# Second chunk's rows loaded uncast between the weight quarters, rows re-ordered at their cast, weight halves crossed over in bf16, work of the first step re-ordered

## The chip, the cores and the metric

The kernel runs on one core of a Trainium2 chip. The metric is the device time of one execution in microseconds (us). Every run quoted is of state fast unless it says otherwise, and its mean granted TensorE clock is given where it matters. PE is the matmul engine, DVE the vector engine, ACT the scalar engine, POOL is GpSimd, SP issues DMAs. A DMA lands when its data have arrived. An eviction is the copy that takes a result of PE to where the next operation reads it.

## The reference

```python
# x: (8, 4096, 192) fp32; weight: (8 heads, 7 taps); w_in: (192, 2048); w_out: (2048, 192); beta: (2048,)
w = exp(weight - max); w = w / (sum(w) + 1e-9)            # softmax over the 7 taps of a head
conv = causal 7-tap convolution of x along the sequence, one set of taps per head of 24 columns
h = conv @ w_in
out = (h * sigmoid(beta * h)) @ w_out                     # 32768 x 192, fp32
```

## The kernel before

The batch is worked in two halves side by side, in steps. Steps 0 and 1 are the two half-chunks (256 tokens) of chunk 0; step 2 is chunk 1 (512 tokens), and so on to step 32. A step has 16 units; a unit multiplies one block of 128 hidden columns (`hidden`), lets ACT apply the activation, and does a quota of output matmul pairs. From chunk 2 on, x comes transposed through DRAM. For the first two chunks that would be too late, so they are transposed on PE:

```python
    x0 = setup.tile([128, NB, 2, D], FP32)      # chunk 0, loaded fp32 by SP
    x0b = setup.tile([128, NB, 2, D], BF16)
    x1b = setup.tile([128, NB, 2, D], BF16)     # chunk 1, cast to bf16 by its DMA
    ...
    def load_x1(h):                             # issued from POOL after the first weight cast
        nc.gpsimd.dma_start(out=x1b[:, :, h, :], in_=x_v[0, TOK : 2 * TOK, h, :].rearrange(...))
    ...
    def cast_w_in(i):                           # POOL: half of weight quarter i
        nc.gpsimd.tensor_copy(w_in_s[:, :, i*FW : i*FW + FH], w_in_raw[:, :, i, :])
    def cross_w_in(i):                          # DVE: the other half, moved across partitions
        for r in range(2):
            nc.vector.tensor_copy(
                w_in_s[(1 - r)*DG : (2 - r)*DG, :, i*FW + FH : (i+1)*FW],
                w_in_raw[r*DG : (r+1)*DG, :, i, :])
    def scale_w_out(i):                         # POOL, right behind cast_w_in(i): 128 x 768 multiply
        ...
    # one transpose for each 64-column group AND each half: 6 for a block of 128 tokens
```

Chunk 0 is convolved on PE with diagonal matrices (7 matmuls a column group). Chunk 1 and all later ones are convolved on DVE: 21 taps a step (7 taps for each of three groups of 64 columns; a tap is one DVE instruction), popped from a queue between the units. What is slipped into the units of step 0 is given by a table:

```python
    first_work = {
        0: lambda: (first_xt(), cross_w_in(1)),
        2: more(xt1_work),              # chunk 1: transposes of its first two blocks
        3: lambda: cross_w_in(2),
        4: more(xt1_work),              # chunk 1: the other two, and the copy to xt
        6: more(conv1_work),            # chunk 0, second half: convolution on PE, group by group
        7: lambda: cross_w_in(3),
        8: more(conv1_work),
        11: more(conv1_work),
    }
    quota = {0: 2, 1: 4, 2: 6, 3: 6, 4: 7}   # output pairs per unit, 8 from step 5 on
    pops = {0: 8, 1: 14, 2: 26}              # DVE taps popped in a step
```

Of the kernel before, what the change touches and what calls it, by code (L numbers as in the profile page):

```python
# [9 lines left out]
FP32 = mybir.dt.float32  # L10
FP32R = mybir.dt.float32r
BF16 = mybir.dt.bfloat16
AF = mybir.ActivationFunctionType
ALU = mybir.AluOpType
# [3 lines left out]
def kernel(  # L18
# [17 lines left out]
    nc = tc.nc  # L36

    B, S, D = x.shape
    H, K = weight.shape
    F = moe_w_in.shape[1]  # L40
    group = D // H
    DG = 64
    NG = D // DG
    TOK = 512
    NF = F // 128
    PAD = K - 1
    HALO = 16
    BLK = 128
# [8 lines left out]
    x_v = x.rearrange("(h p) s d -> p s h d", h=2)  # L57
    out_v = out.rearrange("(h p s) d -> h p s d", h=2, p=B // 2)

    consts = ctx.enter_context(tc.tile_pool(name="consts", bufs=1))  # L60
    setup = ctx.enter_context(tc.tile_pool(name="setup", bufs=1))
# [13 lines left out]
    psum_b = ctx.enter_context(  # L75
        tc.tile_pool(name="psum_b", bufs=1, space=bass.MemoryType.PSUM)
    )
# [3 lines left out]
    def in_a():  # L81
        return psum_a.tile([128, 2, TOK], FP32, name="pa")

    def in_b():
        return psum_b.tile([128, 2, TOK], FP32, name="pb")
# [3 lines left out]
    def new_xt(ch):  # L89
        xt = xt_pool.tile([128, NG, HALO + TOK], BF16, name="xt")  # L90
        if ch % CHUNKS == 0:
            nc.vector.memset(xt[:, :, 0:HALO], 0.0)
        xts[ch] = xt
        return xt
# [22 lines left out]
    NB = TOK // BLK  # L117
    HB = NB // 2
    x0 = setup.tile([128, NB, 2, D], FP32)
    x0b = setup.tile([128, NB, 2, D], BF16)  # L120
    x1b = setup.tile([128, NB, 2, D], BF16)



    NW = 4
    FW = F // NW
    FH = FW // 2
    NQ = NF // NW
    w_in_s = consts.tile([128, NG, F], BF16)
    w_in_raw = setup.tile([128, NG, NW, FH], FP32)  # L130
# [2 lines left out]
    w_in_v = moe_w_in.rearrange("(c d) (i r f) -> i r d c f", c=NG, r=2, f=FH)  # L133
    w_out_v = moe_w_out.rearrange("(c p) d -> p c d", p=128)

    def load_x0(b):
        nc.sync.dma_start(out=x0[:, b, :, :], in_=x_v[0, b * BLK : (b + 1) * BLK, :, :])  # L137

    def load_w_in(i):
        for r in range(2):  # L140
            nc.sync.dma_start(  # L141
                out=w_in_raw[r * DG : (r + 1) * DG, :, i, :], in_=w_in_v[i, r]
            )
# [2 lines left out]
        fcs = slice(i * NQ, (i + 1) * NQ)  # L146
        nc.sync.dma_start(out=w_out_raw[:, fcs, :], in_=w_out_v[:, fcs, :])

    def load_x1(h):
        nc.gpsimd.dma_start(  # L150
            out=x1b[:, :, h, :],
            in_=x_v[0, TOK : 2 * TOK, h, :].rearrange("(b q) d -> q b d", q=BLK),
        )

    e8 = setup.tile([H, K + 1], FP32)
    cw8 = setup.tile([H, K], FP32)
    beta_q = setup.tile([NF, 128], FP32)
    nc.scalar.dma_start(out=cw8, in_=weight)
    nc.scalar.dma_start(out=beta_q, in_=moe_beta.rearrange("(c p) -> c p", p=128))
    for b in range(HB):  # L160
        load_x0(b)
    load_w_in(0)
    load_w_out(0)
    for b in range(HB, NB):
        load_x0(b)
    for i in range(1, NW):
        load_w_in(i)
        load_w_out(i)

# [6 lines left out]
    sel = setup.tile([H, NG, 2, DG], FP32)  # L176
# [3 lines left out]
        out=sel,  # L180
        in_=sel,
        compare_op=ALU.is_ge,
        fill=0.0,
# [5 lines left out]
        out=sel,  # L189
        in_=sel,  # L190
        compare_op=ALU.is_ge,
        fill=0.0,
# [4 lines left out]
    ident = setup.tile([128, 128], FP32)  # L197
# [3 lines left out]
    def cast_w_in(i):  # L201
        nc.gpsimd.tensor_copy(  # L202
            w_in_s[:, :, i * FW : i * FW + FH], w_in_raw[:, :, i, :]
        )

    def cross_w_in(i):
        for r in range(2):
            nc.vector.tensor_copy(  # L208
                w_in_s[(1 - r) * DG : (2 - r) * DG, :, i * FW + FH : (i + 1) * FW],
                w_in_raw[r * DG : (r + 1) * DG, :, i, :],  # L210
            )

    def w_in_of(h, j, fc):
# [7 lines left out]
    def scale_w_out(i):  # L221
        fcs = slice(i * NQ, (i + 1) * NQ)
        nc.gpsimd.tensor_tensor(  # L223
            w_out_s[:, fcs, :],
            w_out_raw[:, fcs, :],
            beta_r[:, fcs].unsqueeze(2).to_broadcast((128, NQ, D)),
            ALU.mult,
        )
# [6 lines left out]
    nc.scalar.activation(warm, warm, AF.Silu)  # L235
    ident_b = setup.tile([128, 128], BF16)
    nc.vector.tensor_copy(ident_b, ident)
    pf = psum_h.tile([128, 2, TOK], FP32, name="ph")

    def fill(n):  # L240
        for _ in range(n):
            nc.tensor.matmul(pf[:, 0, :], zeros[:, 0:128], zeros, start=True, stop=True)  # L242

    fill(5)
    pq = in_a()[:, 0, 0 : NG * (K + 1)]
    for c in range(NG):
        nc.tensor.matmul(
            pq[:, c * (K + 1) : (c + 1) * (K + 1)],
            sel[:, c, :, :].rearrange("i h d -> i (h d)"),
            e8,  # L250
            start=True,
            stop=True,
        )
    pq = pq.rearrange("p (c k) -> p c k", c=NG)
    fill(1)
    nc.vector.tensor_copy(x0b[:, 0], x0[:, 0])
    rq = setup.tile([128, NG], FP32)
    nc.vector.reciprocal(rq, pq[:, :, K])
    cw = consts.tile([128, NG, K], FP32)
    nc.vector.tensor_tensor(  # L260
        cw, pq[:, :, 0:K], rq.unsqueeze(2).to_broadcast((128, NG, K)), ALU.mult
    )
    nc.vector.tensor_copy(x0b[:, 1], x0[:, 1])

    diag = setup.tile([128, NG, K, 128], FP32R)

    def diag_v(c):
        nc.vector.tensor_tensor(
            diag[:, c, :, :],
            ident.unsqueeze(1).to_broadcast((128, K, 128)),  # L270
            cw[:, c, :].unsqueeze(2).to_broadcast((128, K, 128)),
            ALU.mult,
        )

    def transposes(pt, xb, b0, at, nb):
        for b in range(nb):
            for c in range(NG):
                for h in range(2):
                    nc.tensor.transpose(  # L279
                        pt[h * DG : (h + 1) * DG, c, (at + b) * BLK : (at + b + 1) * BLK],  # L280
                        xb[:, b0 + b, h, c * DG : (c + 1) * DG],
                        ident_b,
                    )

    xt0 = setup.tile([128, NG, HALO + TOK], FP32R)
    nc.vector.memset(xt0[:, :, 0:HALO].bitcast(FP32), 0.0)
    cts = {}
# [12 lines left out]
    n0 = HB * BLK  # L300
    for b in range(HB):
        pool, name = (psum_b, "pb") if b == 0 else (psum_a, "pa")
        pt = pool.tile([128, NG, BLK], BF16, name=name)
        transposes(pt, x0b, b, 0, 1)
        nc.scalar.copy(xt0[:, :, HALO + b * BLK : HALO + (b + 1) * BLK], pt)
    pb = in_b()[:, 0, 0:NF]
    nc.tensor.transpose(pb, beta_q, ident[0:NF, 0:NF])
    fill(1)
    diag_v(0)
    diag_v(1)  # L310
    beta = consts.tile([128, NF], FP32)
    nc.vector.tensor_copy(beta, pb)
    nc.vector.reciprocal(beta_r, beta)
    for k in range(K):
        nc.scalar.mul(diag[:, 2, k, :], ident, cw[:, 2, k : k + 1])
    cross_w_in(0)
    cast_w_in(0)
    for h in range(2):
        load_x1(h)
    scale_w_out(0)  # L320
    for i in range(1, NW):
        cast_w_in(i)
        scale_w_out(i)
    ct = ct_pool.tile([128, NG, TOK], BF16, name="ct")
    cts[0] = ct
    for c in range(NG):
        pv = psum_h.tile([128, 2, TOK], FP32, name="ph") if c < 2 else in_a()
        pv = pv[:, 0, 0:n0]
        for k in range(K):
            diag_tap(0, c, k, pv)  # L330
        if c < 2:
            nc.vector.tensor_copy(ct[:, c, 0:n0], pv)
        else:
            nc.scalar.copy(ct[:, c, 0:n0], pv)
    nc.vector.tensor_copy(x0b[:, HB:NB], x0[:, HB:NB])

    def first_xt():
        pt = psum_b.tile([128, NG, n0], BF16, name="pb")
        transposes(pt, x0b, HB, 0, HB)
        nc.vector.tensor_copy(xt0[:, :, HALO + n0 :], pt)  # L340

    def first_conv():
        cts[1] = ct_pool.tile([128, NG, TOK], BF16, name="ct")
        pv = psum_b.tile([128, 4, n0], FP32, name="pb")
        for c in range(NG):
            for k in range(K):
                diag_tap(1, c, k, pv[:, c, :])
            if c == NG - 1:
                nc.vector.tensor_copy(cts[1][:, :, 0:n0], pv[:, 0:NG, :])  # L349
            yield  # L350

    def second_xt():
        xt = new_xt(1)
        pt = psum_b.tile([128, NG, TOK], BF16, name="pb")
        for b in range(NB):
            transposes(pt, x1b, b, b, 1)
            if b % 2 == 0:
                continue
            if b == NB - 1:
                nc.vector.tensor_copy(  # L360
                    xt[:, :, HALO - PAD : HALO], xt0[:, :, HALO + TOK - PAD :]
                )
                nc.vector.tensor_copy(xt[:, :, HALO:], pt)  # L363
            yield

    cast(2)
    cast(3)
# [124 lines left out]
    def more(work):  # L492
        return lambda: next(work, None)

    first_work = {
        0: lambda: (first_xt(), cross_w_in(1)),
        2: more(xt1_work),
        3: lambda: cross_w_in(2),
        4: more(xt1_work),
        6: more(conv1_work),  # L500
        7: lambda: cross_w_in(3),
        8: more(conv1_work),
        11: more(conv1_work),
    }



    quota = {0: 2, 1: 4, 2: 6, 3: 6, 4: 7}
    pops = {0: 8, 1: 14, 2: 26}
    queue = deque()  # L510
    for s in range(N_ST):
        if s + 2 < N_ST:
# [48 lines left out]
```

## Time and profile before

| | before |
|---|---|
| time, median (4 runs) | 704.49 us (704.37 to 705.06) |
| the traced run | 701.91 us, mean granted clock 0.998 |
| PE / DVE / ACT busy, share of the span | 98% / 79% / 83% |
| first unit of step 2 reaches ACT (timeline) | 44.87 us |

From 45 us on PE is busy almost all the time (45 to 100 us: 54.71 of 55); what can still be won is the start. These are lines of the chain of waits of the kernel before (start, duration, what), followed back from the matmul that opens step 2:

```profile
8.39 10.32 DMA x1b<-in_x_dram
...
18.75 0.85 PE pb L279 x11
...
28.27 1.04 PE pb L292 x7
...
29.34 0.96 DVE ct L349
30.30 3.31 DVE ct L382 x5
...
34.67 4.63 DVE ct L382 x7
...
40.36 2.05 DVE ct L382 x4
...
42.93 1.42 DVE ct L382 x2
44.34 0.04 issue
44.38 0.39 PE ph L398 x2
```

Read upwards: step 2's first hidden group is completed at 44.38 by the last DVE taps (L382); they stand in line behind the eviction of chunk 0's convolution (L349), that behind PE's last convolution group (L292), and that behind the transposes of chunk 1 (L279), which waited for the cast-DMA of x1b until 18.7 us.

The windows view of the same kernel shows what the wait did to PE (columns: window, busy time and count of PE, PE's weight loads, DVE, ACT, POOL, then granted clock, DMA share, GB/s):

```profile
core 0: us, PE busy (x) PEld busy (x) DVE busy (x) ACT busy (x) POOL busy (x), PEclk, DMA share, GB/s
14.30:18.75 4.45, 0.24 (x1) 0.11 (x2) 4.18 (x5) 0.55 (x1) 2.35 (x3) 0.95 1.23 249
18.75:22.06 3.31, 3.31 (x43) 2.33 (x45) 0.00 (x0) 1.38 (x2) 2.59 (x3) 0.56 0.24 64
```

PE worked 0.24 of 4.45 us, and then ran at a clock of 0.56. Three lines of the timeline of before (start, duration, engine, what, and in brackets the idle time before it):

```profile
17.11 1.47 POOL L223 TENSOR_TENSOR w_out_s<-w_out_raw,beta_r 128x768 bf16<-128x768 f32 x1 [1.83 <-DMA w_out_raw<-in_moe_w_out_dram]
17.29 1.31 DVE L360 CAST xt<-xt 128x18 bf16<-128x18 f32 x1
18.75 0.85 PE L279 MATMUL pb<-ident_b,x1b 128*64 128x128 bf16 x11 [2.92 <-DMA x1b<-in_x_dram]
```

The middle line is a copy of 18 elements that took 1.31 us: it ended when POOL's multiply ended. And the group of the crossing on the page of before, eight instructions of 0.9 us in the mean (the copy, its shapes, count, then busy us and mean ns):

```profile
L208 DVE CAST w_in_s<-w_in_raw 64x768 bf16<-64x768 f32 x8 | 7.2, 905 | 0.2
```

### The profile page before, as it was taken

The numbers are of one execution on the slowest core, as the hardware profiler recorded it, in microseconds if no ns is written. First come the engines' busy times: TensorE is split into PE (matmuls) and PEld (weight loads), VectorE is DVE, ScalarE is ACT, GpSimd is POOL, SyncE is SP. The second block draws the span as 40 slices with busy tenths as digits, with TensorE's granted clock in tenths as the row PEclk, the third lists the DMA queues.
The fourth block names the chain that finished last, engine by engine and source line by source line (L and its number), as shares of the span: only waits on it lengthen the run. The fifth ranks groups of instructions, "written<-read, shape, count | busy, mean of one in ns | idle before, by whom it ended". The sixth has DMA issues, their size and how long they took to land.

```text
span 700.2 us, 25076 instructions
## 1 busy us (share of the span) xinstructions
PE 688.7 (98%) x11464; PEld 504.6 (72%) x11464; DVE 554.1 (79%) x938; ACT 580.5 (83%) x546; POOL 67.5 (10%) x79
## 2 busy tenths in 40 slices
PE   7999999999999999999999999999999999999997
PEld 5776677777777777777777777777777777777777
DVE  7699999989779877779877778877778977777222
ACT  4689998888888888888888888888888888888882
POOL 5835454000000000000000000000000000000000
PEclk9999999999999999999999999999999999999999
DMA  9999999922231222321223221232221322211111
GB/s 220 124 165 167 166 174 174 143 59 65 65 59 45 62 59 70 58 60 47 58 61 70 59 60 49 57 58 70 60 59 56 50 63 66 60 44 39 37 47 59
DMA packets 184955, 55.38 MB, mean 79 GB/s; under 512 B 147456, under 2 KB 184848, under 8 KB 184848
## 3 DMA queue, kind: packets, MB, share of 16 engines
q0 software_dynamic: 96768, 12.53, 27.8%
q1 hardware_dynamic: 88032, 41.24, 25.4%
q8 instruction: 89, 1.46, 0.9%
q14 instruction: 18, 0.15, 0.1%
q10 hardware_dynamic: 48, 0.01, 0.0%
HBM read 28.98 MB, written 37.29 MB: 95 GB/s over the span
## 4 chain that ended last, share of the span: by engine, by line
PE 94%; DVE 2%; DMA 2%; issue 0%; SPq 0%; ACT 0%; POOL 0%; POOLq 0%
PE ph L398 46%; PE pa L426 24%; PE pb L426 24%; DVE ct L382 2%; DMA x1b<-in_x_dram 1%; DMA w_in_raw<-in_moe_w_in_dram 1%; PE pb L292 0%; DVE osb L445 0%; DVE osb L444 0%; PE pb L279 0%; DVE ct L349 0%; SPq L137 0%; POOL w_in_s L202 0%; SPq L141 0%; ACT g L405 0%
## 5 line engine op out<-in xcount | busy, mean ns | idle before, releaser
L405 ACT ACTIVATE g<-ph,beta 128x1024 bf16<-128x1024 f32 (+1 forms) x528 | 573.3, 1088 | 101.4 <-PE ph L398 95.2
L426 PEld LDWEIGHTS <-g 64*128 64x128 bf16 x8192 | 354.2, 94 | 119.6 <-issue 0.8
L398 PE MATMUL ph<-ct,w_in_s 64*128 64x512 bf16 (+1 forms) x3168 | 419.5, 370 | 0.7 <-DVE ct L382 0.3
L382 DVE SCALAR_TENSOR_TENSOR ct<-xt,cw,ct 128x512 bf16<-128x512 bf16 x558 | 377.2, 744 | 0.0
L426 PE MATMUL pa<-w_out_s,g 64*128 64x192 bf16 x4128 | 217.2, 243 | 0.9 <-issue 0.6
L426 PE MATMUL pb<-w_out_s,g 64*128 64x192 bf16 x4064 | 211.4, 243 | 0.0
L398 PEld LDWEIGHTS <-w_in_s 64*128 64x128 bf16 x3168 | 147.0, 94 | 62.0 <-issue 2.1
L444 DVE COPY osb<-pa 128x384 f32<-128x384 f32 x64 | 35.6, 557 | 99.2 <-PE pa L426 96.2
L104 POOL DMA_DIRECT2D xd<-in_x_dram x60 | 54.5, 911 | 46.8 <-DMA xd<-in_x_dram 45.7
L444 DVE COPY osb<-pb 128x384 f32<-128x384 f32 x63 | 35.1, 557 | 26.2 <-PE pb L426 20.6
L445 DVE TENSOR_TENSOR osb<-pa,osb 128x384 f32<-128x384 f32 (+1 forms) x65 | 36.0, 554 | 3.3 <-ACT osb L442 1.1
L445 DVE TENSOR_TENSOR osb<-pb,osb 128x384 f32<-128x384 f32 x64 | 35.5, 554 | 2.7 <-ACT osb L442 0.5
L380 DVE TENSOR_SCALAR ct<-xt,cw 128x512 bf16<-128x512 bf16 x93 | 28.4, 359 | 0.0
L208 DVE CAST w_in_s<-w_in_raw 64x768 bf16<-64x768 f32 x8 | 7.2, 905 | 0.2
L442 ACT COPY osb<-pb 128x192 f32<-128x192 f32 x1 | 0.3, 319 | 8.1 <-PE pb L426 8.1
L223 POOL TENSOR_TENSOR w_out_s<-w_out_raw,beta_r 128x768 bf16<-128x768 f32 x4 | 6.0, 1488 | 2.9 <-DMA w_out_raw<-in_moe_w_out_dram 2.8
L279 PE MATMUL pb<-ident_b,x1b 128*64 128x128 bf16 x24 | 1.7, 270 | 4.5 <-DMA x1b<-in_x_dram 4.5
L279 PEld LDWEIGHTS <-x1b 128*64 128x64 bf16 x24 | 1.1, 140 | 5.1 <-DMA x1b<-in_x_dram 4.8
L242 PE MATMUL ph<-zeros 128*128 128x512 bf16 x7 | 3.5, 622 | 1.3 <-DVE warm L173 1.3
L202 POOL CAST w_in_s<-w_in_raw 128x768 bf16<-128x768 f32 x4 | 3.3, 836 | 5.1 <-DMA w_in_raw<-in_moe_w_in_dram 5.0
L363 DVE COPY xt<-pb 128x1536 bf16<-128x1536 bf16 x1 | 1.0, 957 | 3.6 <-PE pb L279 3.6
L292 PE MATMUL ph<-xt,diag 128*128 128x256 f32 x14 | 3.4, 434 | 0.0
(52 smaller groups left out, 39.7 us busy)
## 6 DMA issues: line engine op xcount, KB each, us to landing
out_dram<-osb SPq DMA_DIRECT2D x127, 192.0 KB, 2.1
xd<-in_x_dram POOLq DMA_DIRECT2D x54, 198.0 KB, 14.5
w_in_raw<-in_moe_w_in_dram SPq DMA_DIRECT2D x8, 192.0 KB, 5.6
w_out_raw<-in_moe_w_out_dram SPq DMA_DIRECT2D x4, 384.0 KB, 7.7
xd<-in_x_dram POOLq DMA_DIRECT2D x6, 192.0 KB, 15.6
x<-in_x_dram SPq DMA_DIRECT2D x4, 192.0 KB, 2.6
xt<-xd SPq DMA_TRANSPOSE x30, 4.4
x1b<-in_x_dram POOLq DMA_DIRECT2D x2, 192.0 KB, 9.2
```

The costliest lines, as they stand in the source:

```text
L104: nc.gpsimd.dma_start(out=xd[r0:, :, h, :], in_=x_v[p, t0:t1, h, :].rearrange("t (c d) -> t c d", c=NG),)
L208: nc.vector.tensor_copy(w_in_s[(1 - r) * DG : (2 - r) * DG, :, i * FW + FH : (i + 1) * FW], w_in_raw[r * DG : (r + 1) * DG, :, i, :],)
L223: nc.gpsimd.tensor_tensor(w_out_s[:, fcs, :], w_out_raw[:, fcs, :], beta_r[:, fcs].unsqueeze(2).to_broadcast((128, NQ, D)), ALU.mult,)
L242: nc.tensor.matmul(pf[:, 0, :], zeros[:, 0:128], zeros, start=True, stop=True)
L292: nc.tensor.matmul(pv, diag[:, c, k, :], xt0[:, c, o : o + n], start=(k == 0), stop=(k == K - 1),)
L380: nc.vector.tensor_scalar_mul(dst, src, scalar)
L382: nc.vector.scalar_tensor_tensor(out=dst, in0=src, scalar=scalar, in1=dst, op0=ALU.mult, op1=ALU.add)
L398: nc.tensor.matmul(ph[:, h, 0:n], w_in_of(h, j, fc), cts[s][rows, j, 0:n], start=(j == 0), stop=(j == NG - 1),)
L405: nc.scalar.activation(gs[s][:, fc, :, 0:n], ph[:, :, 0:n], AF.Silu, scale=beta[:, fc : fc + 1])
L426: nc.tensor.matmul(self.po[:, r, b * D : (b + 1) * D], g[rows, fc, self.h, q * BLK : (q + 1) * BLK], w_out_s[rows, fc, :], start=(self.don ...
L444: nc.vector.tensor_copy(dst, self.po[:, 0, 0 : nb * D])
L445: nc.vector.tensor_tensor(dst, self.po[:, 1, 0 : nb * D], dst, ALU.add)
```

## The change

The intent: get rid of the slow cast-DMA for chunk 1, halve the transposes, and make the crossing cheaper. Chunk 1's rows are loaded fp32 by SP ahead of the last weight quarter and cast by DVE, which at the same time puts the two halves' columns side by side, so that one transpose serves both halves. The crossing reads the bf16 half that POOL has just cast. The convolution diagonals use the un-normalised exponentials, and the normalisation moves to the eviction. And step 0's table is re-ordered.

```diff
-    x0b = setup.tile([128, NB, 2, D], BF16)
-    x1b = setup.tile([128, NB, 2, D], BF16)
+    x1 = setup.tile([128, NB, 2, D], FP32)
+    x0b = setup.tile([128, NB, NG, 2, DG], BF16)
+    x1b = setup.tile([128, NB, NG, 2, DG], BF16)
+    def cast_rows(xb, x, b0, nb):          # DVE, one copy for each half (cut)
@@ loads on SP
     for i in range(1, NW):
+        if i == NW - 1:
+            for b in range(NB):
+                load_x(x1, TOK, b)
         load_w_in(i)
         load_w_out(i)
@@ crossing
-                w_in_raw[r * DG : (r + 1) * DG, :, i, :],
+                w_in_s[r * DG : (r + 1) * DG, :, i * FW : i * FW + FH],
@@ transposes: one for both halves
-                for h in range(2):
-                    nc.tensor.transpose(pt[h * DG : (h + 1) * DG, c, ...], xb[:, b0 + b, h, c * DG : (c + 1) * DG], ident_b)
+        nc.tensor.transpose(pt, xb[:, b, c].rearrange("q h d -> q (h d)"), ident_b)
@@ first convolution: diagonals from exp alone; evictions multiply by rn = 1 / sum   (cut)
-            cw[:, c, :].unsqueeze(2).to_broadcast((128, K, 128)),
+            eu[:, c, 0:K].unsqueeze(2).to_broadcast((128, K, 128)),
@@ step 0
-        2: more(xt1_work),
-        3: lambda: cross_w_in(2),
-        4: more(xt1_work),
-        6: more(conv1_work),
-        7: lambda: cross_w_in(3),
-        8: more(conv1_work),
-        11: more(conv1_work),
+        2: more(conv1_work),
+        4: lambda: (more(conv1_work)(), cross_w_in(2)),
+        6: lambda: (more(conv1_work)(), cast_rows(x1b, x1, 0, NB)),
+        8: more(xt1_work),
+        9: lambda: (more(xt1_work)(), cross_w_in(3)),
-    pops = {0: 8, 1: 14, 2: 26}
+    pops = {0: 5, 1: 16, 2: 26}
```

More of the change, by code (lines that the diff above doesn't have):

```diff
@@ L119 @@
     x0 = setup.tile([128, NB, 2, D], FP32)
-    x0b = setup.tile([128, NB, 2, D], BF16)
-    x1b = setup.tile([128, NB, 2, D], BF16)
+    x1 = setup.tile([128, NB, 2, D], FP32)
+    x0b = setup.tile([128, NB, NG, 2, DG], BF16)
+    x1b = setup.tile([128, NB, NG, 2, DG], BF16)
+    def cast_rows(xb, x, b0, nb):
+        if nb == 1:
+            nc.vector.tensor_copy(
+                xb[:, b0].rearrange("q c h d -> q h c d"),
+                x[:, b0].rearrange("q h (c d) -> q h c d", c=NG),
+            )
+            return
+        for h in range(2):
+            nc.vector.tensor_copy(
+                xb[:, b0 : b0 + nb, :, h, :],
+                x[:, b0 : b0 + nb, h, :].rearrange("q b (c d) -> q b c d", c=NG),
+            )
     NW = 4
@@ L134, with load_x @@
     w_out_v = moe_w_out.rearrange("(c p) d -> p c d", p=128)
-    def load_x0(b):
-        nc.sync.dma_start(out=x0[:, b, :, :], in_=x_v[0, b * BLK : (b + 1) * BLK, :, :])
+    def load_x(dst, t0, b):
+        t = t0 + b * BLK
+        nc.sync.dma_start(out=dst[:, b, :, :], in_=x_v[0, t : t + BLK, :, :])
     def load_w_in(i):
@@ L147, in load_w_out @@
         nc.sync.dma_start(out=w_out_raw[:, fcs, :], in_=w_out_v[:, fcs, :])
-    def load_x1(h):
-        nc.gpsimd.dma_start(
-            out=x1b[:, :, h, :],
-            in_=x_v[0, TOK : 2 * TOK, h, :].rearrange("(b q) d -> q b d", q=BLK),
-        )
     e8 = setup.tile([H, K + 1], FP32)
@@ L160 @@
     for b in range(HB):
-        load_x0(b)
+        load_x(x0, 0, b)
     load_w_in(0)
@@ L164 @@
     for b in range(HB, NB):
-        load_x0(b)
+        load_x(x0, 0, b)
     for i in range(1, NW):
+        if i == NW - 1:
+            for b in range(NB):
+                load_x(x1, TOK, b)
         load_w_in(i)
@@ L237 @@
     nc.vector.tensor_copy(ident_b, ident)
+    sel_r = setup.tile([H, NG, 2, DG], FP32R)
+    nc.vector.tensor_copy(sel_r, sel)
+    e8r = setup.tile([H, K + 1], FP32R)
+    nc.vector.tensor_copy(e8r, e8)
     pf = psum_h.tile([128, 2, TOK], FP32, name="ph")
@@ L242, in fill, with spread @@
             nc.tensor.matmul(pf[:, 0, :], zeros[:, 0:128], zeros, start=True, stop=True)
-    fill(5)
-    pq = in_a()[:, 0, 0 : NG * (K + 1)]
-    for c in range(NG):
-        nc.tensor.matmul(
-            pq[:, c * (K + 1) : (c + 1) * (K + 1)],
-            sel[:, c, :, :].rearrange("i h d -> i (h d)"),
-            e8,
-            start=True,
-            stop=True,
-        )
-    pq = pq.rearrange("p (c k) -> p c k", c=NG)
-    fill(1)
-    nc.vector.tensor_copy(x0b[:, 0], x0[:, 0])
-    rq = setup.tile([128, NG], FP32)
-    nc.vector.reciprocal(rq, pq[:, :, K])
-    cw = consts.tile([128, NG, K], FP32)
-    nc.vector.tensor_tensor(
-        cw, pq[:, :, 0:K], rq.unsqueeze(2).to_broadcast((128, NG, K)), ALU.mult
-    )
-    nc.vector.tensor_copy(x0b[:, 1], x0[:, 1])
+    NK = NG * (K + 1)
+    def spread(dst, sel, e8):
+        for c in range(NG):
+            nc.tensor.matmul(
+                dst[:, c * (K + 1) : (c + 1) * (K + 1)],
+                sel[:, c, :, :].rearrange("i h d -> i (h d)"),
+                e8,
+                start=True,
+                stop=True,
+            )
+    fill(5)
+    pc = in_a()
+    spread(pc[:, 0, :], sel_r, e8r)
+    for b in range(HB):
+        cast_rows(x0b, x0, b, 1)
+    eu = setup.tile([128, NG, K + 1], FP32)
+    nc.vector.tensor_copy(eu.rearrange("p c k -> p (c k)"), pc[:, 0, 0:NK])
     diag = setup.tile([128, NG, K, 128], FP32R)
@@ L270, in diag_v, with transposes @@
             ident.unsqueeze(1).to_broadcast((128, K, 128)),
-            cw[:, c, :].unsqueeze(2).to_broadcast((128, K, 128)),
+            eu[:, c, 0:K].unsqueeze(2).to_broadcast((128, K, 128)),
             ALU.mult,
         )
-    def transposes(pt, xb, b0, at, nb):
-        for b in range(nb):
-            for c in range(NG):
-                for h in range(2):
-                    nc.tensor.transpose(
-                        pt[h * DG : (h + 1) * DG, c, (at + b) * BLK : (at + b + 1) * BLK],
-                        xb[:, b0 + b, h, c * DG : (c + 1) * DG],
-                        ident_b,
-                    )
+    def transposes(pt, xb, b, c):
+        nc.tensor.transpose(pt, xb[:, b, c].rearrange("q h d -> q (h d)"), ident_b)
     xt0 = setup.tile([128, NG, HALO + TOK], FP32R)
@@ L303 @@
         pt = pool.tile([128, NG, BLK], BF16, name=name)
-        transposes(pt, x0b, b, 0, 1)
+        for c in range(NG):
+            transposes(pt[:, c, :], x0b, b, c)
         nc.scalar.copy(xt0[:, :, HALO + b * BLK : HALO + (b + 1) * BLK], pt)
-    pb = in_b()[:, 0, 0:NF]
+    pq = in_b()[:, 0, :]
+    pb = pq[:, 64 : 64 + NF]
     nc.tensor.transpose(pb, beta_q, ident[0:NF, 0:NF])
+    spread(pq, sel, e8)
     fill(1)
     diag_v(0)
+    rn = setup.tile([128, NG], FP32)
+    nc.vector.reciprocal(rn, eu[:, :, K])
     diag_v(1)
@@ L314 @@
     for k in range(K):
-        nc.scalar.mul(diag[:, 2, k, :], ident, cw[:, 2, k : k + 1])
-    cross_w_in(0)
-    cast_w_in(0)
-    for h in range(2):
-        load_x1(h)
-    scale_w_out(0)
-    for i in range(1, NW):
+        nc.scalar.mul(diag[:, 2, k, :], ident, eu[:, 2, k : k + 1])
+    for i in range(NW):
         cast_w_in(i)
         scale_w_out(i)
+    cross_w_in(0)
     ct = ct_pool.tile([128, NG, TOK], BF16, name="ct")
@@ L331 @@
         if c < 2:
-            nc.vector.tensor_copy(ct[:, c, 0:n0], pv)
+            nc.vector.tensor_scalar_mul(ct[:, c, 0:n0], pv, rn[:, c : c + 1])
         else:
-            nc.scalar.copy(ct[:, c, 0:n0], pv)
-    nc.vector.tensor_copy(x0b[:, HB:NB], x0[:, HB:NB])
+            nc.scalar.mul(ct[:, c, 0:n0], pv, rn[:, c : c + 1])
+    cast_rows(x0b, x0, HB, HB)
+    cw = consts.tile([128, NG, K], FP32)
+    pq = pq[:, 0:NK].rearrange("p (c k) -> p c k", c=NG)
+    rq = setup.tile([128, NG], FP32)
+    nc.vector.reciprocal(rq, pq[:, :, K])
+    nc.vector.tensor_tensor(
+        cw, pq[:, :, 0:K], rq.unsqueeze(2).to_broadcast((128, NG, K)), ALU.mult
+    )
     def first_xt():
         pt = psum_b.tile([128, NG, n0], BF16, name="pb")
-        transposes(pt, x0b, HB, 0, HB)
+        for b in range(HB):
+            for c in range(NG):
+                transposes(pt[:, c, b * BLK : (b + 1) * BLK], x0b, HB + b, c)
         nc.vector.tensor_copy(xt0[:, :, HALO + n0 :], pt)
@@ L343, in first_conv @@
         cts[1] = ct_pool.tile([128, NG, TOK], BF16, name="ct")
-        pv = psum_b.tile([128, 4, n0], FP32, name="pb")
+        pv = in_b().rearrange("p r (c t) -> p (r c) t", t=n0)
         for c in range(NG):
@@ L348, in first_conv @@
             if c == NG - 1:
-                nc.vector.tensor_copy(cts[1][:, :, 0:n0], pv[:, 0:NG, :])
+                nc.vector.tensor_tensor(
+                    cts[1][:, :, 0:n0],
+                    pv[:, 0:NG, :],
+                    rn.unsqueeze(2).to_broadcast((128, NG, n0)),
+                    ALU.mult,
+                )
             yield
@@ L353, in second_xt @@
         xt = new_xt(1)
+        nc.vector.tensor_copy(
+            xt[:, :, HALO - PAD : HALO], xt0[:, :, HALO + TOK - PAD :]
+        )
         pt = psum_b.tile([128, NG, TOK], BF16, name="pb")
         for b in range(NB):
-            transposes(pt, x1b, b, b, 1)
-            if b % 2 == 0:
-                continue
+            for c in range(NG):
+                transposes(pt[:, c, b * BLK : (b + 1) * BLK], x1b, b, c)
             if b == NB - 1:
-                nc.vector.tensor_copy(
-                    xt[:, :, HALO - PAD : HALO], xt0[:, :, HALO + TOK - PAD :]
-                )
                 nc.vector.tensor_copy(xt[:, :, HALO:], pt)
-            yield
+            if b % 2 == 1:
+                yield
     cast(2)
```

## The prediction

> **What bounds it now.** Only the first 45 us of a 700.2 us span can change. From 45 us on the windows view shows PE busy 100% at full clock, one unit of 16 every 1.31 us later, and that code is untouched. So the question is when step 2 (the first 512-token chunk) starts.
>
> In the chain of waits step 2's first hidden group is completed at 44.38 us, released by the last convolution tap on DVE; PE had reached it at 43.1. Behind it: the second chunk's cast-DMA (x1b, 10.3 us, landing at 18.7), its PE transposes, three convolution groups on PE (1.04 us each) until 29.3, eviction 0.96 us, then DVE taps (0.67 us each back to back) and two output evictions (1.1 us each). In the timeline PE idles from 14.0 to 18.75 us for x1b but for one transpose (windows: 0.24 of 4.45 us busy); then the granted clock is 0.56 until 22 us. DVE idles from 18.6 to 22.2 and 26.4 to 29.3.
>
> **What the change does.**
> - x1 comes in fp32 ahead of the last weight quarter: the wait for x1b (4.5 us) goes, and the cold clock with it (about 1.5 us more). The same 786 KB are read; loads already fill 2 to 19 us at 220 to 320 GB/s, so the last quarter lands at 19 to 21 us, as before or 1 us later. It is needed at about 24.
> - Transposes 48 to 24: about 24 x 0.045 = 1.1 us of PE, half of it in idle time.
> - The crossing reads bf16: the Trainium skill, "VectorE: DVE Perf Modes" (side-by-side table), allows four elements a cycle for 16-bit copies within SBUF. The fp32 form took 0.69 to 1.57 us (median 0.83) x8; I estimate 0.35. The skill's "SBUF — State Buffer" (two separate sides) calls the port pair of DVE and GpSimd an exclusive lock; the trace agrees (an 18-element copy took 1.3 us beside GpSimd's multiply), so some crossings will still take over 1 us.
> - Added on DVE: two casts of x1, about 0.6 us each (one of 768 elements took 0.58). The fp32 spread (1.4 us of PE) moves behind the first transposes. Crossing 0 no longer holds up the first evictions, but the first convolution ends near 12 us either way: units start within 0.7 us of before.
> - Step 0: first-chunk convolution in units 2, 4, 6, then x1 cast, transposes in 8 and 9.
>
> **Sum.** Units start at about 12.7. A unit costs 0.66 us (ACT), 0.9 more with a convolution group: convolution done near 20, eviction and casts until 22.2, PE waits about 1.3 us there, xt ready near 24.3, third crossing 25. PE could start step 2 at 38.7. DVE has 21 taps (13.2 us) and two output evictions (2.2 us) from 25: done at 40.4. DVE stays the limit, so about 4 us of the 6 to 7 that PE gets are kept: step 2's first unit near 40.7 (before 44.9). Step 3's taps need the transposed chunk 2, landing near 38: just in time.
>
> 704.6 - 4.2 = 700.4 us; 8 in 10: 697.8 to 702.8. Faster over 2% 0.01, within 2% 0.985, slower 0.005.
>
> **Signs.** No PE wait for x1b; granted clock near 1.0 from 12 us on; crossings near 0.35 us; a short PE wait for the x1b cast near 21 us; step 2's first unit near 40.7 us, still released by a DVE tap; steady stage unchanged.
>
> **What would make it wrong.** The last weight quarter or x1 landing late (2 us less, or no gain); a clock that warms during the first taps (1 us more); GpSimd locking out the casts; transposed chunk 2 later than 40 us, which moves the stall to step 3.

## The result

The changed kernel took 700.16 us in the median (698.63 to 700.85, 4 runs) against 704.49 us for the kernel before. The ratio is 0.9934, with a 95% interval of 0.9915 to 0.9953. A ratio is always the mean time of one kernel's fast runs over that of the other's fast runs of the same rounds, so it is not quite the ratio of the medians quoted. Later runs of both, in the same rounds, gave 700.51 against 703.61 us, ratio 0.9956 (0.9935 to 0.9976). The output was correct.

The traced run of the changed kernel took 700.69 us. Its chain of waits to the start of step 2:

```profile
12.20 8.36 DMA x<-in_x_dram
...
20.75 1.04 DVE x1b L133 x2
...
21.83 0.51 PE pb L292 x6
...
24.41 0.80 DVE w_in_s L221
...
25.24 0.97 DVE w_in_s L221
...
26.23 1.67 DVE ct L407 x3
...
30.28 5.30 DVE ct L409 x8
...
36.63 5.31 DVE ct L409 x8
41.94 0.04 issue
41.98 0.61 PE ph L425 x2
```

The convolution group of chunk 0 has gone from the chain, and step 2's first group is completed at 41.98 instead of 44.38. But x1 lands at 20.6 us, which is *later* than x1b did before (18.7). So an earlier arrival of the rows cannot be what gained the time. The last two lines also say that DVE is still the limit. The windows view of the changed kernel:

```profile
14.30:18.75 4.45, 4.45 (x58) 3.73 (x57) 3.21 (x4) 2.72 (x5) 3.77 (x3) 1.00 1.13 275
20.00:22.00 2.00, 0.56 (x13) 0.32 (x8) 1.41 (x4) 1.04 (x2) 0.00 (x0) 1.00 0.93 181
38.00:42.00 4.00, 1.48 (x20) 0.58 (x15) 3.93 (x6) 1.00 (x2) 0.30 (x1) 0.94 1.32 142
42.00:45.50 3.50, 3.50 (x36) 2.39 (x37) 2.19 (x6) 1.74 (x2) 1.65 (x2) 0.58 1.74 161
```

In the stretch in which PE did 0.24 us of work before, it is now busy throughout at full clock. It has two new waits instead, near 20 us for the cast of x1 and from 38 to 42 us for DVE's taps (DVE is busy 3.93 of these 4 us), and after the second one the clock is at 0.58 for 3.5 us: a new cold stretch, just where step 2 begins. Four lines of the timeline of the changed kernel:

```profile
14.27 1.47 POOL L236 TENSOR_TENSOR w_out_s<-w_out_raw,beta_r 128x768 bf16<-128x768 f32 x1 [1.14 <-DMA w_out_raw<-in_moe_w_out_dram]
14.40 1.62 DVE L221 COPY w_in_s<-w_in_s 64x768 bf16<-64x768 bf16 x1
21.83 0.51 PE L292 MATMUL pb<-ident_b,x1b 128*128 128x128 bf16 x6 [1.44 <-DVE x1b L133]
42.69 1.12 ACT L432 ACTIVATE g<-ph,beta 128x1024 bf16<-128x1024 f32 x1 [3.69 <-PE ph L425]
```

And the crossing's group on the page of the changed kernel:

```profile
L221 DVE COPY w_in_s<-w_in_s 64x768 bf16<-64x768 bf16 x8 | 7.7, 965 | 1.6 <-POOL w_in_s L215 1.4
```

In these two traces reading bf16 did not make it cheaper: 965 ns in the mean against 905. That mean is not a constant of the kernel: the second traces, taken later, gave 1170 ns for the kernel before and 614 ns for the changed one.

### The profile page after: what moved, and what is told of

Its sections match the earlier page's. It is cut to its first block, busy times and chain, and to the rows that moved or that the text cites. A ratio compares the mean times of both kernels' runs of the same rounds, so it can differ in the third digit from the quotient of the medians.

```text
span 698.9 us, 25043 instructions
## 1 busy us (share of the span) xinstructions
PE 688.4 (98%) x11442; PEld 504.4 (72%) x11442; DVE 555.6 (79%) x945; ACT 580.6 (83%) x546; POOL 65.9 (9%) x77
## 4 chain that ended last, share of the span: by engine, by line
PE 94%; DVE 3%; DMA 2%; SPq 1%; issue 0%; ACT 0%; DVEq 0%
PE ph L425 46%; PE pa L453 24%; PE pb L453 24%; DVE ct L409 2%; DMA x<-in_x_dram 1%; DMA w_in_raw<-in_moe_w_in_dram 1%; DVE osb L472 0%; SPq L157 0%; SPq L153 0%; DVE w_in_s L221 0%; DVE ct L407 0%; DVE osb L471 0%; DVE x1b L133 0%; PE pb L292 0%; DVE xt L389 0%
## 5 line engine op out<-in xcount | busy, mean ns | idle before, releaser
L471 DVE COPY osb<-pb 128x384 f32<-128x384 f32 x63 | 35.1, 557 | 27.5 <-PE pb L453 22.2
L221 DVE COPY w_in_s<-w_in_s 64x768 bf16<-64x768 bf16 x8 | 7.7, 965 | 1.6 <-POOL w_in_s L215 1.4
L301 PE MATMUL pb<-xt,diag 128*128 128x256 f32 x21 | 3.3, 296 | 0.0
L301 PEld LDWEIGHTS ph<-xt,diag 128*128 128x128 f32 x14 | 3.2, 328 | 0.1
```

Of the source, the lines that this page charges most:

```text
L221: nc.vector.tensor_copy(w_in_s[(1 - r) * DG : (2 - r) * DG, :, i * FW + FH : (i + 1) * FW], w_in_s[r * DG : (r + 1) * DG, :, i * FW : i * ...
L301: nc.tensor.matmul(pv, diag[:, c, k, :], xt0[:, c, o : o + n], start=(k == 0), stop=(k == K - 1),)
L471: nc.vector.tensor_copy(dst, self.po[:, 0, 0 : nb * D])
```

## The experiments

Theory A, formed from these traces: the gain comes from the new order of step 0. In the old order PE reaches chunk 1's transposes in units 2 and 4, long before any load can deliver, and everything behind them waits, chunk 0's convolution too. In the new order that convolution fills the time. Theory B, which is what the prediction says: the uncast load ahead of the last quarter removes the wait. Rival C: the cheaper transposes, the crossing and the earlier first convolution give it.

### Before, again

The kernel before, unchanged.

> The kernel before, unchanged, to see its own scatter: the traced run of before took 701.9 us, its other runs 704.4 to 705.1. If the cold-clock stretch after the wait for x1b varies from run to run, spans differ by 1 to 3 us while nothing else does; if not, all lie within 0.5 us of 704.5. Ratio to before 1.000.

Measured: 704.44 us (703.12 to 705.3), ratio 1.0007 (0.9993 to 1.0022). Its trace was of a run of 703.53 us, clock 0.995. The scatter is real and the clock goes with it: of the 11 runs of the kernel before in these rounds, one was at 0.998 (702.02 us), the others at 0.992 to 0.995 (702.7 to 705.3 us). The first trace of before (0.998, 701.91 us) was thus of a rare, good run. The windows view of this second trace of before:

```profile
14.30:18.75 4.45, 0.32 (x1) 0.13 (x1) 4.36 (x4) 0.54 (x1) 2.81 (x3) 0.76 1.24 259
16.00:24.00 8.00, 4.06 (x50) 2.90 (x52) 4.15 (x5) 1.37 (x2) 5.59 (x6) 0.57 0.53 121
```

Here x1b landed at 20.2 us, 1.5 us later than in the first trace, and the clock was low for most of 16 to 24 us. The first unit of step 2 reached ACT at 46.50 us instead of 44.87. So it is not the clock alone that varies: the landing does too.

### The order alone

```diff
 (the kernel before, with nothing but)
-        2: more(xt1_work),  3: lambda: cross_w_in(2),  4: more(xt1_work),
-        6: more(conv1_work), 7: lambda: cross_w_in(3), 8: more(conv1_work), 11: more(conv1_work),
+        2: more(conv1_work), 4: lambda: (more(conv1_work)(), cross_w_in(2)), 6: more(conv1_work),
+        8: more(xt1_work),   9: lambda: (more(xt1_work)(), cross_w_in(3)),
-    pops = {0: 8, 1: 14, 2: 26}
+    pops = {0: 5, 1: 16, 2: 26}
```

> Kernel before with nothing but the new order of step 0 (first chunk's convolution in units 2, 4, 6, second chunk's transposes in 8 and 9, crossings at 0, 4, 9; quotas of taps 5 and 16). x1b still comes by the cast-DMA and lands near 18.7 us. Theory A (the order hides the wait: in the changed kernel x1 lands later than x1b did, at 20.6 us, so the load cannot be the gain): 699 to 701 us, as fast as the whole change or faster, no PE wait for x1b. Theory B (the uncast load is what removes the wait, as the prediction put it): within 1.5 us of before, 703 to 705.

Measured: 699.06 us (698.45 to 699.65, 6 runs) against 704.0 for before in the same rounds, ratio 0.9932 (0.9919 to 0.9944). That is the whole gain of the change, from its smallest part. (The numbers of taps popped in steps 0 and 1 moved together with the table; the two were not tested apart.) Lines of its chain of waits, and its windows view where before had stalled:

```profile
8.40 12.38 DMA x1b<-in_x_dram
...
20.82 0.52 PE pb L279 x11
...
35.20 5.31 DVE ct L382 x8
40.51 0.04 issue
40.55 0.61 PE ph L398 x2
```

```profile
14.00:20.00 6.00, 5.87 (x75) 4.96 (x75) 4.45 (x6) 3.40 (x7) 4.09 (x3) 1.00 1.20 242
```

The cast-DMA lands at 20.8 us, two microseconds later than in the first trace of before, and costs PE 0.2 us in waits, because PE had 5.87 us of other work in these 6. Theory A holds, theory B is refuted as the main cause.

### The load alone

```diff
 (the kernel before, old order; load_x1 by cast-DMA taken out)
+        if i == NW - 1:                       # ahead of the last weight quarter, on SP, fp32
+            for b in range(NB): nc.sync.dma_start(out=x1[:, b, :, :], in_=...)
@@ second_xt
+        for h in range(2): nc.vector.tensor_copy(x1b[:, 2*h : 2*h + 2], x1[:, 2*h : 2*h + 2])
```

> Kernel before with nothing but the uncast load of x1 ahead of the last weight quarter, cast on DVE ahead of its transposes in unit 2; old order. Theory A: PE waits in unit 2 until x1 has landed near 20.5 us and is cast, so no gain or a loss of 1 to 3 us: 704 to 708 us. Theory B: 700 to 702 us.

Measured: 702.33 us (700.49 to 703.44), ratio 0.9978 (0.9961 to 0.9994). Neither expectation is met in full: it gains about 1.5 us where theory A expected none. In its trace x1 landed in two parts, the first cast at 16.8 us and the second at 18.7, and PE waited 3.5 us. So with the old order, an uncast load is a small help, a third of the change's gain. The traced run is one of the two fastest of the six.

### The change without its load

```diff
 (the changed kernel)
-            load_x(x1, TOK, b)               # SP, fp32
+            nc.gpsimd.dma_start(out=x1b[:, :, h, :], ...)      # POOL, cast-DMA, as before
-        6: lambda: (more(conv1_work)(), cast_rows(x1b, x1, 0, NB)),
+        6: more(conv1_work),                 # x1b transposed in halves again
```

> Changed kernel with x1 again by the cast-DMA (its transposes in halves again, no cast on DVE), everything else as changed. Theory A: as fast as the changed kernel or up to 2 us faster (x1b lands near 18.7, DVE has 1 us less, the last weight quarter lands near 19 instead of 22.5): 698 to 700.5 us. Theory B: the wait for x1b is back, 703 us or more.

Measured: 699.65 us in the median of its five fast runs (698.01 to 702.24), ratio 0.9943 (0.9922 to 0.9964). The sixth run, the traced one, was slow (1026.71 us at a clock of 0.657), so its trace says nothing. It was run again beside the changed kernel:

> The kernel of undo_load again, since its one trace fell into a run at a clock of 0.66. Theory A: median 698 to 700.5 us, not slower than changed_again; scatter of 3 to 4 us because the cast-DMA's landing varies (18.7 to 24.2 us in the traces so far), against 2 to 3 us for the changed kernel. If the uncast load were worth a real gain: 1 us or more slower than changed_again.

> The changed kernel again, for its scatter and to stand beside the three below on one chip: 698.6 to 701 us; runs whose mean granted clock is 1.000 near 698.6, runs at 0.998 near 700.5, if the difference is the cold clock at the start of step 2.

Measured in the same rounds: 699.16 us (697.62 to 700.79), ratio 0.9933 (0.9912 to 0.9955), without the uncast load; 700.51 us (699.59 to 702.25), ratio 0.9956 (0.9935 to 0.9976), with it. With the new order in place the uncast load gains nothing. If anything it loses a microsecond, but the intervals overlap. The scatter, 3.2 us without the uncast load and 2.7 with it, lies in the two expected ranges, but six runs each are too few to tell them apart. The clock's part of the expectation for the changed kernel held only roughly: its one run at 1.000 took 699.89 us, and one at 0.998 took 699.59.

### The change without its order

```diff
 (the changed kernel, with the old table and taps)
+        2: lambda: (cast_rows(x1b, x1, 0, NB), more(xt1_work)()),
+        3: lambda: cross_w_in(2),  4: more(xt1_work),  6: more(conv1_work),
+        7: lambda: cross_w_in(3),  8: more(conv1_work), 11: more(conv1_work),
+    pops = {0: 8, 1: 14, 2: 26}
```

> Changed kernel with step 0 in the old order and the old tap quotas (8 and 14); load uncast, rows re-ordered at the cast, one transpose for both halves, crossing in bf16, normalisation at the eviction all as changed. Theory A (order is the whole gain): 702 to 704.5 us, PE waiting 2 to 4 us for the x1 cast in unit 2. Rival C (the cheaper transposes, the bf16 crossing and the earlier first convolution give the gain): within 1 us of the changed kernel, 699.5 to 701.

Measured: 703.95 us (702.7 to 706.82), ratio 1.0006 (0.9986 to 1.0025). Without the new order the whole rest of the change is worth nothing; rival C falls. The timeline of this run shows why:

```profile
22.09 0.82 PE L292 MATMUL pb<-ident_b,x1b 128*128 128x128 bf16 x6 [8.19 <-DVE x1b L133]
```

PE stood still for 8.19 us, more than the 2 to 4 expected; the trace is of the second slowest of the six runs (706.18 us). Here x1 landed at 21.0 us, and `cast_rows` copies one half of all four blocks at a time, so it waits for the last of them. In the trace of the load alone the cast of the first two blocks began at 16.8 us already, and the last ones had landed at 18.7. So of the 4.2 us between the first casts, about 1.9 go with the form of the cast and 2.3 with the later landing. SP issued the loads 1.0 us later here (9.84 against 8.85 us); the rest was not settled, and one trace is of one of its kernel's two fastest runs, the other of one of its two slowest.

### The crossing

Theory D: the bf16 crossing must now follow POOL's cast, and right behind that cast POOL starts its multiply of 1.5 us, for which DVE's copy must wait. Two experiments: read fp32 again, and cut the multiply in four.

```diff
 (undo_cross: the changed kernel with)
-                w_in_s[r * DG : (r + 1) * DG, :, i * FW : i * FW + FH],
+                w_in_raw[r * DG : (r + 1) * DG, :, i, :],
```

> Changed kernel with the crossing read from the fp32 weights again. Theory D (the bf16 crossing gained nothing: it must now follow GpSimd's cast, just where GpSimd starts its 1.5 us multiply, and waits for it): crossings again about 0.8 us in the mean against 0.97, time 699.5 to 700.8 us, as changed. Theory E (the prediction: bf16 halves the crossing): slower than changed by 1 to 3 us, 701 to 703.

Measured: 700.29 us (698.81 to 702.44), ratio 0.9947 (0.9932 to 0.9963). As the changed kernel; the crossings took 959 ns in the mean. The bf16 crossing as placed gained no time that can be measured, and theory E (the prediction's) falls. The expected 0.8 us was not met: two of the eight fp32 copies overlapped a multiply of POOL and took 1.58 and 1.65 us, and the shortest took 0.68.

```diff
 (scale_pieces: the changed kernel with)
-        nc.gpsimd.tensor_tensor(w_out_s[:, fcs, :], w_out_raw[:, fcs, :], ..., ALU.mult)   # NQ = 4 blocks
+        for f in range(i * NQ, (i + 1) * NQ): nc.gpsimd.tensor_tensor(w_out_s[:, f : f + 1, :], ..., ALU.mult)
```

> Changed kernel with GpSimd's multiply of a weight quarter cut in four pieces of about 0.4 us each, same arithmetic. If crossings are slow because DVE waits for a whole GpSimd multiply (theory D): crossings fall from 0.97 us to 0.5 to 0.7 in the mean, step 2 starts near 41.2 instead of 42.0 us, time 0.3 to 1 us below changed. If they are slow for another reason (shape, 64 partitions): mean stays above 0.85 us and the time is that of the changed kernel.

Measured: 698.93 us (698.55 to 700.72), ratio 0.9933 (0.9919 to 0.9947), about 1.2 us below the changed kernel's 700.16 of other rounds, with overlapping intervals. Four of its six runs had a clock of 1.000, against two of the ten of the changed kernel (698.63 and 699.89 us), so the difference may be the clock's. The groups of this run:

```profile
L237 POOL TENSOR_TENSOR w_out_s<-w_out_raw,beta_r 128x192 bf16<-128x192 f32 x16 | 8.0, 528 | 1.7 <-DMA w_out_raw<-in_moe_w_out_dram 1.7
L221 DVE COPY w_in_s<-w_in_s 64x768 bf16<-64x768 bf16 x8 | 3.8, 480 | 2.2 <-POOL w_in_s L215 2.0
```

The crossing fell to 480 ns, from 965 and 614 in the two traces of the changed kernel, without being touched itself; the two later kernels with the cut multiply gave 574 and 493. Theory D holds for the long copies: those of 1.64, 1.62 and 1.44 us in the changed kernel each began within 0.4 us of a multiply, and alone the copy takes 0.42. (In the trace of undo_order, where it mostly fell clear of the multiplies, the mean was 479 ns too.) It is not the whole story for the last crossing, which stands ahead of the taps: its second copy (25.24 us, 0.97 us long) began after the multiply had ended and ran beside POOL's DMA issues, which follow from 24.87 us on.

### Filling the wait before step 2

PE waits for DVE's taps at the start of step 2, and the clock can go cold there. A larger output quota in step 1 gives PE work to do meanwhile, first on the kernel with the order alone:

```diff
-    quota = {0: 2, 1: 4, 2: 6, 3: 6, 4: 7}
+    quota = {0: 2, 1: 5, 2: 6, 3: 6, 4: 7}
```

> Kernel before with the new order alone, and output quota 5 instead of 4 pairs a unit in step 1, so that PE does 16 more output pairs (0.16 us each, 2.6 us) where it only waited for DVE's last taps (36.9 to 40.5 us in the trace of the order alone), and the clock does not go cold there. If DVE's taps are what step 2 waits for (theory A, second half): step 2 starts no later, PE waits under 1 us there, granted clock 1.0 at 40 to 44 us, and the time falls by 2.5 to 4 us below the order alone: 695 to 697 us. If PE were the limit there: no change, 699 us.

Measured: 698.0 us (697.57 to 702.63, 6 runs), ratio 0.9926 (0.9905 to 0.9947). The typical run, four of the six, is at 697.6 to 698.1: about 1.2 us below the order alone, not the 2.5 to 4 expected. (The order alone was run in other rounds, and the intervals of the two ratios overlap, so this small gain is not shown.) The trace fell in the one slow-starting run (702.63 us), in which x1b landed at 24.2 us, so the new order is not proof against a late cast-DMA.

> Changed kernel with the multiply in four pieces and output quota 5 in step 1. order_quota5 gained 1.3 us over the order alone, less than the 2.5 to 4 expected. If only the cold clock was saved and the pulled-forward output pairs turned into a wait for DVE's taps at the start of step 3: about 697.5 to 698.5 us, PE waiting for taps 1 to 3 us between 55 and 64 us, clock 1.0 throughout. If pulled-forward work counts in full: 695 to 696.5 us.

Measured: 698.25 us (697.14 to 699.66), ratio 0.9921 (0.9903 to 0.994), clock 1.000 in all six runs, against 700.51 us for the changed kernel in the same rounds. The first expectation is met in time and clock: the cold stretch is gone. Its wait is not: PE is busy 3.48 of the 4 us from 60 to 64, at the start of step 3, so it waits 0.5 us there and not 1 to 3, and what it waits for is an output eviction that stands behind 17 taps in DVE's queue. Most of what the pulled-forward output was to save was lost elsewhere. From the first unit of step 2 on ACT to the first of step 3, PE had 154 output matmuls in this trace and 186 in that of scale_pieces, 32 fewer (the 16 pairs, 2.6 us by the expectation), and yet the step took 17.27 against 18.02 us. ACT was busy for 16.84 of these 17.27 us, which points to ACT as the limit there; this was not tested.

Last, x1 was loaded before the third quarter of w_out, and cast in unit 4:

```diff
 (pieces_quota5, with)
-        if i == NW - 1: (the four load_x of x1, ahead of load_w_in; cut)
         load_w_in(i)
+        if i == NW - 2:
+            for b in range(NB): load_x(x1, TOK, b)
         load_w_out(i)
-        6: lambda: (more(conv1_work)(), cast_rows(x1b, x1, 0, NB)),
+        4: lambda: (more(conv1_work)(), cross_w_in(2), cast_rows(x1b, x1, 0, NB)),   6: more(conv1_work),
```

> As pieces_quota5, with x1 loaded before the third quarter of w_out instead of after it, and cast in unit 4, before the eviction of the first convolution. x1 lands near 19.0 instead of 20.6 us, so PE no longer waits 1.4 us for the cast and DVE's tap chain starts 0.7 us earlier: 0.5 to 1 us below pieces_quota5 if DVE's chain sets the start of steps 2 and 3; the same if it does not.

Measured: 696.85 us (696.36 to 697.41, 5 runs), ratio 0.9901 (0.9882 to 0.992): the best version, 3.7 us below the changed kernel's median of the same rounds and 6.8 below before's. It is 1.4 us below pieces_quota5, more than the 0.5 to 1 expected, though the intervals of the two ratios overlap (the slowest of its five runs took 697.41 us, the fastest of the other six 697.14). Its timeline and its chain of waits:

```profile
17.27 1.03 DVE L133 CAST x1b<-x 128x768 bf16<-128x768 f32 x2 [0.37 <-issue]
```

```profile
44.81 11.26 DVE ct L410 x17
...
58.19 0.48 DVE osb L472
...
59.30 0.50 PE pa L454 x8
```

The cast began at 17.3 us without waiting for data (20.75 in the changed kernel): x1 landed earlier than the 19.0 expected. Now the chain runs through 17 taps of step 3 and the output eviction behind them, which is the next thing to work on.

## Why the prediction was right, and where it was not

The time was right: 700.4 predicted, 700.16 measured. That it came so close is luck: two of its reasons were wrong, and two errors of size cancelled. A table of the traced runs (without the slow one of undo_load) shows the sizes; "rest" is time minus the first unit of step 2, both of the same run:

| traced run | time, us | first unit of step 2 on ACT, us | rest, us |
|---|---|---|---|
| before | 701.91 | 44.87 | 657.0 |
| before_again | 703.53 | 46.50 | 657.0 |
| load_only | 700.54 | 43.76 | 656.8 |
| undo_order | 706.18 | 49.41 | 656.8 |
| order_only | 699.53 | 41.26 | 658.3 |
| changed | 700.69 | 42.69 | 658.0 |
| changed_again | 699.59 | 42.82 | 656.8 |
| undo_load_again | 700.79 | 42.10 | 658.7 |
| undo_cross | 698.81 | 42.05 | 656.8 |
| scale_pieces | 698.55 | 41.79 | 656.8 |
| order_quota5 | 702.63 | 46.12 | 656.5 |
| pieces_quota5 | 699.66 | 43.37 | 656.3 |
| early_x1 | 696.36 | 40.13 | 656.2 |

- **Only the start can change, and the question is when step 2 starts: right.** Of the ten runs with the old quota the rest is 656.8 to 657.0 us in seven, whatever the kernel. In order_only, changed and undo_load_again it is 1.2 to 1.9 us more than 656.8, and these are the three whose windows show a clock of 0.57 to 0.58 just behind the start of step 2. Step 2 itself, from its first unit on ACT to the first of step 3, took 19.2 to 19.7 us in these three and 18.0 in the other seven. The larger quota takes off only 0.3 to 0.6 us of rest, so it gained less than expected.
- **"x1 comes in fp32 ahead of the last weight quarter: the wait for x1b goes": the wrong cause.** This is the step that failed. What the order alone shows is that the wait goes when chunk 1's transposes move from units 2 and 4 to 8 and 9, behind chunk 0's convolution: PE then worked 5.87 of the 6 us from 14 to 20, although x1b landed at 20.8. The order alone gave 0.9932, the change without the order 1.0006, and the change without the load was no slower than with it. The prediction listed the new order as its last item, without a gain of its own, although its sum already used it ("convolution done near 20, eviction and casts until 22.2").
- **"The crossing reads bf16 ... I estimate 0.35": wrong where it stood.** It measured 965 ns in the mean in the first trace and 614 in the second (before: 905 and 1170). The shortest copies took 0.42 us, so the estimate of the copy was nearly right, and the wait it would meet was underrated. The prediction did say that "some crossings will still take over 1 us", and three of the eight did in the first trace. There the third crossing ended at 26.2 us instead of 25.
- **"DVE stays the limit, done at 40.4": right limit, 1.5 us too early.** The taps ended at 41.9. The third crossing, which stands ahead of them, was 1.2 us late, and the first three taps took 1.67 us rather than 1.08 (three of the 359 ns that such a tap took in the mean before). PE was done with step 1 near 38.6, as predicted (38.7).
- **"Granted clock near 1.0 from 12 us on": wrong.** The prediction removed the wait and its cold clock, and did not charge the new wait from 38 to 42 us with the same price: 0.58 for 3.5 us, 1.0 to 1.2 us of time by the table.
- **The wait for the cast near 21 us, 1.3 us: right** (1.44 us).
- **What cancelled.** From trace to trace step 2 starts 2.2 us earlier (44.87 to 42.69), not 4.2, and 1.0 of that is lost again to the cold clock, so the two traced runs differ by only 1.2 us. But the trace of before is of a rare good run. The typical run of before has a mean clock of 0.992 to 0.995; the second trace shows such a one, and there step 2 starts at 46.50. The prediction started from the median of the times and took its saving from the better trace, and the two errors made up for each other.

## What to carry to other kernels

When an in-order engine waits for a load, look first for independent work further back in its own program that can stand ahead of the wait; here this alone, a change of a table, gave as much as the whole change (0.9932 against 0.9934), and the new load path, the fewer transposes and the narrower copy gave nothing without it (1.0006). A copy made cheaper can gain nothing, as here, if its new input puts it right next to a long instruction of the other engine for which it has to wait. And where times scatter, take the traced run's own time and clock before subtracting anything: a saving read from a lucky trace is not the saving of the median.

## What the Trainium skill lacked or had wrong

- "TensorE: Matmul & The Clock Gate" (HAM oscillation) gives the rule that PE must not idle for more than about 3.4 us. Here the longest single idle time before the clock fell to 0.58 was 2.06 us, in a stretch of 4 us in which PE was busy for 1.48; in another run of the same kernel a single idle time of 1.94 us near 20 us was followed by 0.50. So gaps shorter than the rule's went with a lost clock, in some runs and not in others: in scale_pieces PE was busy for only 1.75 of the 4 us from 38 to 42, and the clock stayed at 1.00. The page does say, in other sections, that the window runs free, that the effect varies from run to run, and that frequent short idle times can cost the clock too; what it lacks is how much idle time within a window is enough, and these runs do not settle it.
- "SBUF — State Buffer" (two separate sides) calls the port pair of DVE and GpSimd an exclusive lock held for a whole instruction. The runs bear it out: the same crossing took 0.42 us alone and 1.62 us when a multiply of 1.47 us had started 0.13 us ahead of it (a full wait would have made 1.47 - 0.13 + 0.42 = 1.76, so they agree roughly). The page lacks a remedy that helped here: cut GpSimd's instruction (four of 0.53 us in place of one of 1.49), which costs GpSimd 0.6 us a quarter and brought the mean crossing to 0.48 to 0.57 in three traces.
- "VectorE: DVE Perf Modes" (side-by-side table) allows four 16-bit elements a cycle and an overhead of about 150 cycles, by which 768 elements should take about 0.36 us (an estimate from that page). The shortest crossing took 0.418 us, a little more.
- No page that was read gives the scatter of a cast-DMA's landing: 10.3, 11.8, 11.9, 12.4 and 14.8 us from issue for the same 192 KB piece in five traces. Its cause was not looked for.
